# A gated long-convolution and spectral-filter kernel: a written-out order replaced, an output chunk kept in SBUF, zero matmuls ahead of the first data

## The chip, the cores and the metric

One core of a Trainium2 chip runs the whole program. TensorE (PE in the profile) does the matmuls, with its weight loads shown apart as PEld; VectorE (DVE), ScalarE (ACT) and GpSimd (POOL) work on tiles; SyncE (SP) issues most of the transfers, and GpSimd issues those that add to what DRAM already holds. The metric is the device time of one execution in microseconds; lower is better. The profile's times are counted from the start of the profiled span.

## The reference

Inputs are `q`, `k`, `v` and `x = q` of 2048 tokens by 640 channels (float32), and two branches are mixed by a gate of one number per token:

```python
def _A_ref(q, k, v, shift_k, ssm_k, ssm_D):
    k_shift = sum over t of k_pad[:, t:t + S, :] * shift_k[:, ks - 1 - t]   # 4 taps
    kv = k_shift * v
    y = irfft(rfft(kv, 2 * S) * rfft(ssm_k, 2 * S))[:S]     # long causal convolution, per channel
    return q * (y + kv * ssm_D)
def _B_ref(x, w_r, w_i):
    return irfft2(rfft2(x) * (w_r + 1j * w_i))               # over tokens and channels
g = _sigmoid((x * gate_w).sum(-1, keepdims=True))
return g * a + (1 - g) * b
```

## The kernel before

All transforms are matmuls with constant matrices. The 640 channels, in an order `PERM`, make five chunks of 128. The 2048 tokens are written as 64 x 2 x 16; a block `n` of 0 to 15 holds the 128 tokens with one last index, and blocks 0 to 7 and 8 to 15 are the two halves.

Branch B, in order: `dfwd(n)` loads a block of `xT`, folds it by symmetric channels (`fold`: sums and differences on DVE and POOL, one scaled copy on ACT) and multiplies by the channel matrix `dfc`, result in `XX`. Two unused columns of `dfc` are filled at run time by `gate_cols` with the gate's weights, so the same matmuls give the gate's sums; `gate` turns these into `g` and into `om`, which holds 1-g and g-1. `b1` and `bs2` are the two token steps forward with the product by `w`; `i1` the first step back; `bfin(n)` the last: matmuls `u` (L479, L485), a copy on ACT, matmuls `dic` (L497, L501). `bout(n)` scales by `om`, makes a sum (322 columns) and a difference (318) and sends the 128 x 640 block out.

Branch A, per chunk `c`: `kv` (four taps, transposes on PE, product with `v`), `s1` ("H" for the filter, "Y" for the data), `amid` (second step, product with the filter), `is1a` (first step back) and `afin(c, n0)` (last step back for one half of the blocks, product with `q*g`). The complex product of `amid` leaves four real products. `is1a` either takes all four as separate matmuls, or, for chunks in `SUMP`, `asum` first adds them in pairs on DVE or POOL and `is1a` has half the matmuls (`inv1`, L297).

The output of both branches is summed in DRAM. `FIRST` says, per half, from which chunk on branch B is the one that is written first. Before, `FIRST = (4, 5)`: chunks 0 to 3 of blocks 0 to 7, and all five chunks of blocks 8 to 15, are stored by `afin` and then added to by `bout` with GpSimd's accumulating transfer (L524); chunk 4 of blocks 0 to 7 is stored by `bout` (L522) and added to by `afin` (L681). An accumulating transfer waits until the store under it has landed.

Nothing is scheduled by the compiler. [...] There are 11 buffers `a`, 5 `s`, one `k`, one `kvt`, one `c1`, three `z` and the 8 PSUM banks.

Of the kernel before, what the change touches and what calls it, by code (L numbers as in the profile page):

```python
# [5 lines left out]
F32 = mybir.dt.float32  # L6
# [20 lines left out]
10/4/0 14/4 11 12 13 15 16 17 73+1/2/1 77/6 74+1 76+1 109+1/4/3 113/0 75+1 110+1 112<110 179/10 143 78 64+1/0/2 65+1 66+1 67<66 79 312/0 18/1 318/2  # L27
309/3 305/4 27/4 114 68/2 69 70 145+1/1/0 146+1 148<146 147 306 80 149/6 150 151 71 111 115 307 308/5 296/0 55/2/1 59/2 60 56 57+1 58+1 61 100+1/4/0
313 314/4/0 81/7 152 316/6 301/6 19/2/3 20 21 22+1<21 126/1 116 23/0 24 25 62 104/2 315 45/0 101 102 105 28/1/2 32/4 103+1 106 33 29+1<103 31+1 30+1
34 90/8 317 319+1 322/6 82/4/3 83 85 26 297/0 298 299 300/4 378/0 84 185/7 127/0/1 128 36/1 107 320/2 321 192/2 302/0/0 310/2 224/4 35 86/4 87 88 89  # L30
303 46/2/4 50/0 47 130 311 324/2/1 328/4 323 330/6 379/5 380/6 129 49 51 325 131/2 48 52 331 91/3/2 2 132 133 92+1 93+1 94+1 384/3 95/6 96 97 6 382/0
37/0/4 38 40 39 134 41/2 42 43 381<39 98 383 385 326/6 53 329 44 163/4 164 167/0 168 157/2 165/4 161/0 153 327 159/6 389/0 390/8 395/1 391/6 393/0 392
394 396 8/0 231/3 166 352/4 353/6 355+1 354+1 158 162 160 180/2 181/3/1 182 183 184 348/0 360/6 349/0 351 350 193/2 194/2/4 195 186/4 188/0/1 361/0
363+1 362 196+1 197<196 173/0 174 386/1 387/2/0 388 187/10 189 190+1 356/4 357/3 397/6 336/6 337/2 338 339+1<338 175/0 176 171/2 172 359 358 477/0
478/5 479/0 480 257/1 191 177/0 178 481/7 482 211/10 219/6 220/2/4 221 223 222 244/2 169/2 170 406/0 225/4 227/3/0 226/9 228 229 230 398/0 399 7 154/6
155 400/7 250/8 258/2 259/1/2 260 261 262 344/4 345/6 346+1 347+1 340/6 341/4 343 342 332/0 333/0 334 335 212/2 213/4 214/3/4 215 217 216 276/9 277/6
279/1/2 412/0/2 413 418/2 419 416/4 417 198/1 488/6 278/4 280+1 281<280 282 483/10 466/0 232/0 233/0/3 234 236+1 401+1<236 489+1 407+1 199/2 201/4/1
200/4 202+1 203<202 204 235 468/9 366/4 367 368/3 467/1 469 156 369 484 364/0 365 414/4 415 373/4 251/6 252/9 253/2/1 254 255 256 263/10 470/8 471 374
# [12 lines left out]
681+1 649 831 682/4/0 647 644/0 810 811 746/6/0/1 654 683 645 676 812/4 813 814 678/4 679 832+1/3 833<832 650/0 651 652 684/2 685 687+1 688/4 689
690/0 691 747 692/6/2 696/2 698/4 693 694/0 695 697 748/6 749 750 816/9 736/0/4/3 877/0 878 737 786/2/2/0 699 708/0 720/4 787 712/2 805 751 716/6
752+1/7 753+1 754 709/1 711 710 788/0 755 721/6 723+1<753 722 724/4 717/1 718 719 728/6 765 713/1 714+1<722 715 738/2 725/2 727 726 700/4 789 790 791
704/0 729/6 730 731 862/6/1/2 815 792/7<731 793 794 701/4 702 703 766/4/0/4 739 705/1 707 706 863 864/6 865 740 741 732/0 742/2<706 743 745 866 867
868+1/6 869+1 767 734/4 795 733 768/0 769 655/2 735 823/4 776/6/1/3 770 771 772+1/4 773<772 774 835/0/2/0 656 657 824 825 744 775 817 818/2 819 834
870 836 879 777 778/4 779 780 781 782+1/1 783<782 784 785 837/0 838 839 840 841/7 844/6/4/1 889/2/2/3 861 845 846/4 847 820 842+1 880/0/0/4 843 848
849 850/5<842 851 852 890 891/6 881 882/2 892 893 894 895+1/8 896<895 897 883 884 885 886+1/2 887<886 888
# [154 lines left out]
def _body(ctx, tc, I, out):  # L212
# [21 lines left out]
    def ps(b):  # L234
        return banks[:, b.slot:b.slot + b.banks]
# [38 lines left out]
    gs = cst.tile([128, 12], F32, name="gs")  # L274
# [30 lines left out]
    def gate_cols():  # L305
        unit("gcol")

        def calc():
            xv = gw.rearrange("p (u k) -> p u k", u=2)
            a, b = gs[:, 0:6], gs[:, 6:11]  # L310
# [500 lines left out]
```

## Time and profile before

| | |
|---|---|
| time, median of 3 runs | 312.15 us (310.73 to 313.74) |
| profiled execution: its time, its span | 312.69 us, 310.9 us |
| PE busy | 271.1 us, 87% of the span |
| DVE, POOL, ACT busy | 233.6, 186.8, 135.7 us |
| mean granted TensorE clock | 0.974 |
| DRAM read, written | 43.47 MB, 10.49 MB |
| of it by GpSimd's accumulating transfers | 5.24 MB |

Busy time is a share of the whole span and hides that stages differ; the view by windows gives it for one stretch. The chain of waits is followed back from the last instruction. In a timeline row stand start, length, engine, line, operation, output and inputs, the number of merged instructions, and in brackets how long the engine had been idle before it and who released it. A block's channel-transform matmul shows as x16 because each float32 matmul is two passes.

### The profile page before, as it was taken

What the parts mean: (1) busy time and instruction counts of PE and PEld (TensorE: products, weight loads), DVE (VectorE), ACT (ScalarE), POOL (GpSimd) and SP (SyncE); (2) the same over time, 40 slices, a digit from 0 to 9 for tenths busy, and PEclk for the clock granted to TensorE, in tenths of its full rate; (3) what the DMA queues carried; (4) which work ended last, traced back from release to release, by engine and by line L of the source; (5) the groups of instructions that cost most, each with busy time, mean ns of one, the idle gap of its engine ahead of it and who ended that gap; (6) DMA issues with size and microseconds to landing.
All of it is one profiled execution on the core that took longest, in us unless ns stands there. A gap on an engine that the chain in (4) does not pass through costs nothing. (4 is left out here: it accounts for less than half of the span.)

```text
span 310.9 us, 9643 instructions
## 1 busy us (share of the span) xinstructions
PE 271.1 (87%) x4196; PEld 167.7 (54%) x4196; DVE 233.6 (75%) x293; ACT 135.7 (44%) x229; POOL 186.8 (60%) x171
## 2 busy tenths in 40 slices
PE   0779999999989979979899899899999999999900
PEld 0556657455454345624337576476755767488700
DVE  2578898489979899965899888987789777665230
ACT  2154537614462652466652465766270354033300
POOL 3326794978898798949869615525943154123491
PEclk9999999999999999989999999999999999999965
DMA  7998769525684437959322950004553370436996
GB/s 235 409 409 330 288 214 404 214 69 165 186 278 147 159 103 242 265 205 383 121 95 80 317 186 0 11 2 136 175 189 108 73 99 17 70 89 130 181 130 108
DMA packets 25418, 54.58 MB, mean 176 GB/s; under 512 B 1824, under 2 KB 13344, under 8 KB 24864
## 3 DMA queue, kind: packets, MB, share of 16 engines
q1 hardware_dynamic: 22032, 48.72, 46.0%
q0 software_dynamic: 3344, 5.24, 11.4%
q8 instruction: 33, 0.54, 0.7%
q14 instruction: 9, 0.07, 0.1%
HBM read 43.47 MB, written 10.49 MB: 174 GB/s over the span
## 5 line engine op out<-in xcount | busy, mean ns | idle before, releaser
L559 POOL TENSOR_TENSOR a<-a,a 128x1024 f32<-128x1024 f32 x24 | 57.1, 2380 | 10.1 <-ACT XX L378 4.7
L593 DVE STREAM_TRANSPOSE ZZ<-banks 128x1024 f32<-128x1024 f32 x40 | 47.8, 1228 | 3.4 <-PE banks L590 3.3
L616 PE MATMUL banks<-ZZ,s2a 64*32 64x256 f32 x1280 | 41.4, 389 | 3.8 <-issue 1.7
L553 ACT ACTIVATE a<-k,one 128x1024 f32<-128x1024 f32 x32 | 34.9, 1141 | 13.5 <-DMA k<-k 10.1
L633 POOL TENSOR_TENSOR ZZ<-a 128x512 f32<-128x512 f32 x19 | 24.3, 1290 | 16.9 <-ACT a L625 11.2
L363 PE MATMUL banks<-dfc,s 128*64 128x162 f32 x256 | 22.8, 324 | 12.0 <-DVE dfc L321 9.8
L616 PEld LDWEIGHTS banks<-ZZ,s2a 64*32 64x32 f32 x1280 | 24.2, 105 | 16.8 <-issue 2.9
L297 PE MATMUL banks<-ZZ,one 32*64 32x512 f32 x512 | 30.9, 605 | 0.7 <-DVE ZZ L593 0.4
L631 DVE TENSOR_TENSOR ZZ<-banks,s 128x512 f32<-128x512 f32 x40 | 25.4, 685 | 7.9 <-ACT s L627 7.7
L302 DVE STREAM_TRANSPOSE ZZ<-banks 128x2048 f32<-128x2048 f32 x10 | 23.0, 2312 | 7.4 <-PE banks L297 7.4
L363 PEld LDWEIGHTS banks<-dfc,s 128*64 128x64 f32 x256 | 17.7, 145 | 17.0 <-POOL s L338 9.8
L458 POOL TENSOR_TENSOR XX<-s,s 128x320 f32<-128x320 f32 (+1 forms) x29 | 24.2, 856 | 4.5 <-DVE s L452 2.8
L625 ACT ACTIVATE a<-banks 128x1024 f32<-128x1024 f32 x20 | 20.3, 1024 | 14.9 <-DVE XX L422 7.1
L524 POOL DMA_DIRECT2D out_dram<-a x16 | 15.1, 1022 | 18.5 <-DMA out_dram<-a 10.4
L513 ACT ACTIVATE s<-banks,om 128x322 f32<-128x322 f32 x16 | 8.5, 530 | 39.6 <-PE banks L501 27.5
L518 POOL TENSOR_TENSOR a<-s 128x318 f32<-128x318 f32 x13 | 12.8, 987 | 20.1 <-issue 9.4
L515 DVE SCALAR_TENSOR_TENSOR s<-banks,om,s 128x322 f32<-128x322 f32 x32 | 17.3, 544 | 9.2 <-ACT s L513 8.6
L664 ACT ACTIVATE a<-a,g 128x128 f32<-128x128 f32 x80 | 24.2, 392 | 0.0
L627 ACT ACTIVATE s<-banks 128x512 f32<-128x512 f32 x20 | 12.0, 598 | 23.5 <-PE banks L616 21.2
L501 PE MATMUL banks<-dic,s 128*128 128x161 f32 x128 | 21.9, 313 | 0.0
L501 PEld LDWEIGHTS banks<-dic,s 128*128 128x128 f32 x128 | 18.0, 189 | 7.1 <-issue 7.1
L297 PEld LDWEIGHTS banks<-ZZ,one 32*64 32x64 f32 x512 | 12.9, 129 | 15.6 <-issue 12.9
(73 smaller groups left out, 491.6 us busy)
## 6 DMA issues: line engine op xcount, KB each, us to landing
a<-xT SPq DMA_DIRECT2D x16, 512.0 KB, 7.4
k<-k SPq DMA_DIRECT2D x10, 704.0 KB, 5.9
a<-h SPq DMA_DIRECT2D x10, 544.0 KB, 3.7
a<-w SPq DMA_DIRECT2D x16, 322.0 KB, 3.9
a<-v SPq DMA_DIRECT2D x10, 512.0 KB, 4.8
a<-q SPq DMA_DIRECT2D x10, 512.0 KB, 4.8
out_dram<-a SPq DMA_DIRECT2D x9, 512.0 KB, 3.7
out_dram<-a POOLq DMA_DIRECT2D x8, 320.0 KB, 6.2
```

The source lines that it names most:

```text
L297: mm(p[h * 64:h * 64 + 64, j, :nd * 8], is1[r, c, :], v[r, h * 2 + ri, :, d0:d0 + nd, :].rearrange("p m d e -> p d m e"), start=(i == 0), ...
L302: nc.vector.transpose(by_col(x, d0, nd), p[:, :, :nd * 8].rearrange("p j (d i) -> p d j i", i=8))
L363: mm(v[ri * 64:ri * 64 + 64, z, o], fv[:, i, t], dfc[:, i, :], start=(b == 0), stop=True, tile_position=(0, ri * 64), skip_group_check=True)
L458: either(2 * nc_, lambda q, ri=ri, o=o, dst=dst: q(dst(), T(t1)[:, :, ri], T(t2)[:, :, 1 - ri], op=o), r=[t1, t2], w=[("XXp", z, i, ri)])
L501: mm(ps(p)[:, k, r * 161:r * 161 + 161], sb(u, 5, 128)[:, k * 2 + r], dic[:, (k * 2 + r) * 161:(k * 2 + r) * 161 + 161], start=False, stop ...
L553: tap = lambda t, j: op([("ACT", act_us(1024), lambda: act(sb(t, 8, 128), K(j), AF.Copy, scale=sh[:, c, j:j + 1]))], r=[k, "one"], w=[t], ...
L559: either(1024, lambda o, t=t: o(sb(acc, 1024), sb(acc, 1024), sb(t, 1024), op=OP.add), r=[t], w=[acc])
L593: op([("DVE", dve(1024), lambda: nc.vector.transpose(by_col(Z(z), u * 32, 32), ps(p).rearrange("p b (d n) -> p d b n", n=16)))], r=[p], w= ...
L616: mm(ps(p)[j * 32:j * 32 + 32, h].rearrange("p (y r d) -> p y r d", y=2, r=2)[:, :, ri], s2a[r, k, ri * 32:ri * 32 + 32], ZZ[r, a:b + 1:b ...
L631: alts = [("DVE", dve(512), lambda x=x, dst=dst, hv=hv: tt(dst(), V(part(ps(p), zy)), hv(), op=OP.mult))]
L633: alts.append(("POOL", pool_us(512), lambda x=x, dst=dst, hv=hv: ptt(dst(), V(part(sb(hs, 2, 512), zy)), hv(), op=OP.mult)))
L664: act(sb(qt, 8, 128)[:, j], sb(qt, 8, 128)[:, j], AF.Copy, scale=g[:, n0 + j:n0 + j + 1])
```

## The change

- `FIRST` becomes (4, 4), with `KEEP = (1,)`: branch B no longer adds to chunk 4 of blocks 8 to 15 in DRAM. `bout` leaves these 128 columns of each of the eight blocks in one SBUF tile (`keep`), and the last `afin` takes the product with `q*g` in two halves of 512 columns, adds the kept columns, and stores. To make the kept columns one operation, `PERM` is rearranged and the difference is split into 190 and 128 columns.
- `SUMP` becomes (2, 3, 4): the products of chunk 4 are summed too.
- `warm`: 14 matmuls of a zeroed 128x128 tile stand first on PE; nothing uses their result.
- `gate_cols` writes into `dfc` directly; the factor 0.25 moves into the sigmoid's scale. `gate` makes 1-g as a second sigmoid and g-1 as a scaled copy, all on ACT.
[...]

```diff
-PERM = np.array(list(range(161)) + list(range(320, 481)) + [640 - d for d in range(1, 160)] + [320 - d for d in range(1, 160)])
-FIRST = (4, 5)
-FWD, INV, SUMP = 1, 1, (2, 3)
+PERM = np.array(list(range(161)) + list(range(320, 481)) + [b - d for lo, hi in ((1, 96), (96, 160)) for b in (640, 320) for d in range(lo, hi)])
+FIRST = (4, 4)
+FWD, INV, SUMP = 1, 1, (2, 3, 4)
+WARM = 14
+KEEP = (1,)
 TABLE = """
-117/0 1 0 118+1/0/1 119<118 4 122/0 123 120 121 135/1 136/2/3 140/2 137 139 3 5 124 125 141 9/2 72/3 108/4 63/5 138+1 142 304/0 54/6 144/7 99/8 218/9
+10/0 3 0 2 1/0 5 64/1 118/2 55/3 28/4 312/5 109/6 91/7 304/0 11/0/1 127/8 12 100/9 15/2 46/10 14 136/0 13+1<14 16 6 17 65+1/2/3 66+1 69/4 309/1 67+1
...
-            tt(b[:, 0:2], a[:, 0:6:4], a[:, 1:6:4], op=OP.add)
-            tt(b[:, 2:4], a[:, 0:6:4], a[:, 1:6:4], op=OP.subtract)
-            stt(b[:, 4:5], a[:, 3:4], sg, a[:, 2:3], op0=OP.mult, op1=OP.add)
-        op([("DVE", 0.7, calc)], r=["one", "two"], w=["gs"])
-        def put():
...
+            tt(w[:, 0:323:322], a[:, 0:6:4], a[:, 1:6:4], op=OP.add)
+            tt(w[:, 484:487:2], a[:, 0:6:4], a[:, 1:6:4], op=OP.subtract)
+            for r, j in ((slice(0, 64), 0), (slice(64, 128), 160)):
+                stt(dfc[r, 4, j:j + 1], a[r, 3:4], sg[r], a[r, 2:3], op0=OP.mult, op1=OP.add)
+        op([("DVE", 1.5, calc)], r=["one", "two"], w=["dfc"])
...
-        op([("ACT", 1.5, lambda: act(g, ps(p)[:, 0, :16], AF.Sigmoid))], r=[p], w=["g"])
         def f():
-            nc.vector.tensor_scalar(om[:, 0], g, -1.0, 1.0, op0=OP.mult, op1=OP.add)
-            nc.vector.tensor_scalar(om[:, 1], g, 1.0, None, op0=OP.subtract)
-        op([("DVE", 0.25, f)], r=["g"], w=["om"])
+            act(g, ps(p)[:, 0, :16], AF.Sigmoid, scale=0.25)
+            act(om[:, 0], ps(p)[:, 0, :16], AF.Sigmoid, scale=-0.25)
+            act(om[:, 1], om[:, 0], AF.Copy, scale=-1.0)
+        op([("ACT", 1.9, f)], r=[p], w=["g", "om"])
...
+        either(190, lambda q: dif(q, yn()[:, 322:512], 1, 96), r=rr, use=[ab, y], w=[(y, 1)])
+        if keep:
+            either(128, lambda q: dif(q, sb(keep, 8, 128)[:, n % 8], 96, 160), r=rr, use=[ab, keep], w=[(keep, n)], new=[] if keep in made else [keep])
...
+        fin = c == NCH - 1 and n0 // 8 in kept
+        for i in range(2 if fin else 1):
+            m = 512 if fin else 1024
...
+        if c == NCH - 1 and keep:
+            for i in range(2):
+                r = slice(i * 4, i * 4 + 4)
+                either(512, lambda o, r=r: o(sb(qt, 8, 128)[:, r], sb(qt, 8, 128)[:, r], sb(keep, 8, 128)[:, r], op=OP.add), "DVE", ...)
+                load(lambda r=r: dma(out[:, n0 + r.start:n0 + r.stop, c, :], sb(qt, 8, 128)[:, r]), 262, r=[(qt, "y", i)], use=[qt])
...
+    unit("warm")
+    op([("DVE", 0.2, lambda: nc.vector.memset(wrm, 0.0))], w=["wrm"])
+    pw = new("ps")
+    def warm():
+        for _ in range(WARM):
+            mm(ps(pw)[:, 0, :128], wrm, wrm, start=True, stop=True)
+    pe(6.0, warm, "F", r=["wrm"], w=[pw], new=[pw])
```

Since the table tells nothing by itself, three places in the order follow. In the changed kernel's rows the lines have moved by a few numbers: L596 is the old L590, L571 the old L565, L302 the old L297 on PE, L681 the old L675, L476/L482 the old `u`, L494/L498 the old `dic`, L530 the old L524, L699 the old L681.

The first loads on SP, before:

```order
L332 DMA a_63<-xT 128x1024
L282 DMA two<-two 128x129
L282 DMA one<-one 128x476
L332 DMA a_64<-xT 128x1024
L282 DMA dfc<-dfc 128x972
L332 DMA a_65<-xT 128x1024
```

and in the changed kernel:

```order
L328 DMA a_63<-xT 128x1024
L287 DMA two<-two 128x129
L287 DMA one<-one 128x476
L287 DMA dfc<-dfc 128x972
L328 DMA a_64<-xT 128x1024
L328 DMA a_65<-xT 128x1024
```

The channel matrix `dfc`, which the first matmul needs, has changed places with the second block of `xT`.

The end of PE's list, before: `u` of block 15, `dic` of 10, `u` of 14, `dic` of 15 and 14, all of the second half.

```order
L479 MATMUL banks<-c_79,XX 128x2x64 x4
L485 MATMUL banks<-c_79,XX 32x64 x8
L497 MATMUL banks<-dic,s_78 128x322 x2
L501 MATMUL banks<-dic,s_78 128x161 x4
L479 MATMUL banks<-c_79,XX 128x2x64 x4
L485 MATMUL banks<-c_79,XX 32x64 x8
L497 MATMUL banks<-dic,s_76 128x322 x2
L501 MATMUL banks<-dic,s_76 128x161 x4
L497 MATMUL banks<-dic,s_74 128x322 x2
L501 MATMUL banks<-dic,s_74 128x161 x4
```

In the changed kernel, after the last half of chunk 4's `is1a`: `dic` of block 12, `u` of 14 and 13, `afin(4, 0)` (L681), `dic` of 13 and 14, `afin(4, 8)`:

```order
L494 MATMUL banks<-dic,s_74 128x322 x2
L498 MATMUL banks<-dic,s_74 128x161 x4
L476 MATMUL banks<-c_79,XX 128x2x64 x4
L482 MATMUL banks<-c_79,XX 32x64 x8
L476 MATMUL banks<-c_79,XX 128x2x64 x4
L482 MATMUL banks<-c_79,XX 32x64 x8
L681 MATMUL banks<-ZZ,is2a 64x128 x16
L494 MATMUL banks<-dic,s_74 128x322 x2
L498 MATMUL banks<-dic,s_74 128x161 x4
L494 MATMUL banks<-dic,s_78 128x322 x2
L498 MATMUL banks<-dic,s_78 128x161 x4
L681 MATMUL banks<-ZZ,is2a 64x128 x16
```

Chunk 4's `afin` of blocks 8 to 15 has moved from the middle of the blocks to the very end.

The end of POOL's list, before: adds of the last blocks alternate with the accumulating transfers.

```order
L524 DMA out_dram<-a_73 128x640
L681 DMA out_dram<-a_72 128x8x128
L524 DMA out_dram<-a_70 128x640
L517 TENSOR_TENSOR a_68<-s_75 128x322
L518 TENSOR_TENSOR a_68<-s_75 128x318
L524 DMA out_dram<-a_68 128x640
L518 TENSOR_TENSOR a_71<-s_77 128x318
L524 DMA out_dram<-a_71 128x640
L518 TENSOR_TENSOR a_65<-s_78 128x318
L524 DMA out_dram<-a_65 128x640
```

and in the changed kernel:

```order
L530 DMA out_dram<-a_71 128x512
L530 DMA out_dram<-a_64 128x512
L699 DMA out_dram<-a_67 128x8x128
L516 TENSOR_TENSOR a_65<-s_77 128x128
L516 TENSOR_TENSOR a_73<-s_75 128x190
L530 DMA out_dram<-a_73 128x512
L530 DMA out_dram<-a_63 128x512
L516 TENSOR_TENSOR a_65<-s_76 128x128
```

Each accumulating transfer has 512 columns instead of 640, two stand behind the last `afin` add (L699) instead of four, and the last POOL row fills the kept tile (`a_65` here).

More of the change, by code (lines that the diff above doesn't have):

```diff
@@ L273, in _body @@
     g = cst.tile([128, 16], F32, name="g")
[L274 removed]
+    gs = cst.tile([128, 8], F32, name="gs")
+    wrm = cst.tile([128, 128], F32, name="wrm")
     om = cst.tile([128, 2, 16], F32, name="om")
@@ L466, in i1 @@
         op([("DVE", dve(nd * 32), lambda: back4(XX, ps(p), d0, nd))], r=[p], w=[("XXi", u)])
+    kept, made = {h: new("a") for h in KEEP}, set()
     def bfin(ns, is2b_buf):
@@ L510, in bout @@
         c1 = FIRST[n // 8]
+        keep = kept.get(n // 8)
         av = lambda: sb(ab, 2, 2, 161)
@@ L517, in bout @@
         either(322, lambda q: q(sb(y, 2, 161), av()[:, :, 0], av()[:, :, 1], op=OP.add), r=[(ab, 0), (ab, 1)], use=[ab], w=[(y, 0)], new=[y])
-        either(318, lambda q: q(sb(y, 640)[:, 322:].rearrange("p (a c) -> p a c", a=2), av()[:, :, 0, 1:160], av()[:, :, 1, 1:160], op=OP.subtract),
-               r=[(ab, 0), (ab, 1)], use=[ab, y], w=[(y, 1)])
-        yv = lambda lo, hi: sb(y, NCH, 128)[:, lo:hi]
-        if c1 < NCH:
-            load(lambda: dma(out[:, n, c1:, :], yv(c1, NCH)), 65 * (NCH - c1), r=[(y, 0), (y, 1)], use=[y], w=[("o", c, n // 8, n) for c in range(c1, NCH)])
+        dif = lambda q, o, lo, hi: q(o.rearrange("p (a c) -> p a c", a=2), av()[:, :, 0, lo:hi], av()[:, :, 1, lo:hi], op=OP.subtract)
+        yn = lambda: sb(y, 640)
+        rr = [(ab, 0), (ab, 1)]
+        either(190, lambda q: dif(q, yn()[:, 322:512], 1, 96), r=rr, use=[ab, y], w=[(y, 1)])
+        if keep:
+            either(128, lambda q: dif(q, sb(keep, 8, 128)[:, n % 8], 96, 160), r=rr, use=[ab, keep], w=[(keep, n)], new=[] if keep in made else [keep])
+            made.add(keep)
+        else:
+            either(128, lambda q: dif(q, yn()[:, 512:640], 96, 160), r=rr, use=[ab, y], w=[(y, 2)])
+        yv = lambda lo, hi: sb(y, 640).rearrange("p (c d) -> p c d", d=128)[:, lo:hi]
+        ys = [(y, i) for i in range(2 if keep else 3)]
+        if c1 < NCH and not keep:
+            load(lambda: dma(out[:, n, c1:, :], yv(c1, NCH)), 65 * (NCH - c1), r=ys, use=[y], w=[("o", c, n // 8, n) for c in range(c1, NCH)])
         if c1:
             op([("POOL", 1.0, lambda: nc.gpsimd.dma_start(out[:, n, :c1, :], yv(0, c1), accum_op=OP.add))],
-               r=[(y, 0), (y, 1)] + [("o", c, n // 8, n) for c in range(c1)], use=[y], kb=130 * c1)
+               r=ys + [("o", c, n // 8, n) for c in range(c1)], use=[y], kb=130 * c1)
     def kv(c, h, kvt):
```

82 lines of the change are left out of this document (41 added, 41 removed).

## The prediction

> **What bounds the kernel now.** I read the page's shares first, then the chain that ended last, then windows cut where PE's work changes, then the timeline at both ends.
>
> ```profile
> span 310.9 us, 9643 instructions
> PE 271.1 (87%) x4196; PEld 167.7 (54%) x4196; DVE 233.6 (75%) x293; ACT 135.7 (44%) x229; POOL 186.8 (60%) x171
> PE 27%; POOL 5%; DMA 3%; issue 2%; DVE 2%; POOLq 0%; ACT 0%; ACTq 0%; DVEq 0%
> ```
>
> PE is busy for 87% of the span, and PE has the largest share of the chain, which reaches back only to 176.96 us. Where the other 13% lie shows by stages (columns: window, its length, busy time of PE, PEld, DVE, ACT, POOL, granted clock, DMA share, GB/s):
>
> ```profile
> 9.79:56.24 46.45, 43.93 (x560) 30.07 (x560) 35.63 (x64) 22.94 (x36) 25.87 (x30) 1.00 0.89 344
> 56.24:130.00 73.76, 67.91 (x1186) 36.79 (x1192) 66.09 (x73) 33.52 (x49) 63.04 (x52) 1.00 0.56 175
> 130.00:176.00 46.00, 42.00 (x737) 21.89 (x724) 37.38 (x34) 25.13 (x38) 35.21 (x25) 0.96 0.56 191
> 176.00:240.00 64.00, 61.26 (x900) 39.13 (x901) 53.85 (x63) 32.43 (x68) 31.53 (x28) 1.00 0.34 110
> 240.00:296.05 56.05, 56.04 (x826) 39.74 (x822) 35.41 (x50) 19.63 (x35) 19.63 (x23) 1.00 0.53 96
> 4.36:298.53 294.17, 271.14 (x4196) 167.66 (x4196) 233.58 (x293) 135.73 (x229) 181.88 (x162) 0.99 0.57 177
> ```
>
> The first matmul starts at 9.79, the last ends at 296.05. In between PE lacks 2.5 + 5.9 + 4.0 + 2.7 + 0.0 = 15.1 us; it is 95% busy, and the granted clock stays at 1.00 but for 0.96 in one window. So the span is 9.8 of lead-in + 271.1 of matmuls + 15.1 of PE waits + 14.9 after the last matmul. This sum is the profiled execution's: 310.9 of span in a time of 312.69, 1.8 around it; the median of the runs is 0.5 lower than that execution.
>
> The lead-in and the end:
>
> ```profile
> 2.59 0.43 SPq L282 DMA_DIRECT2D dfc<-dfc  x1
> 7.72 1.26 POOL L337 TENSOR_TENSOR s<-a 128x512 f32<-128x512 f32 x1 [0.38 <-DMA a<-xT]
> 8.95 1.03 DVE L321 TENSOR_SCALAR dfc<-gs 128x2 f32<-128x2 f32 x4 [1.20 <-DMA dfc<-dfc]
> 9.79 2.43 PE L363 MATMUL banks<-dfc,s 128*64 128x162 f32 x16 [9.79 <-DVE dfc L321]
> 12.14 1.36 PE L372 MATMUL banks<-dfc,s 64*64 64x162 f32 x16
> 13.43 1.90 PE L363 MATMUL banks<-dfc,s 128*64 128x162 f32 x16
> 15.26 0.78 PE L372 MATMUL banks<-dfc,s 64*64 64x162 f32 x16
> 15.97 1.32 PE L363 MATMUL banks<-dfc,s 128*64 128x162 f32 x16
> ...
> 276.78 1.23 DVE L678 TENSOR_TENSOR a<-banks,a 128x1024 f32<-128x1024 f32 x1 [0.62 <-PE banks L675]
> ...
> 284.53 2.64 POOL L524 DMA_DIRECT2D out_dram<-a  x3 [7.59 <-DMA out_dram<-a]
> ...
> 290.50 1.10 PE L479 MATMUL banks<-c,XX 128*128 128x128 f32 x8
> 291.89 0.81 PE L497 MATMUL banks<-dic,s 64*128 64x322 f32 x4
> 293.93 0.81 PE L497 MATMUL banks<-dic,s 64*128 64x322 f32 x4
> 294.68 1.37 PE L501 MATMUL banks<-dic,s 128*128 128x161 f32 x8
> 303.28 0.86 POOL L524 DMA_DIRECT2D out_dram<-a  x1 [0.30 <-POOL a L518]
> ```
>
> At the start DVE waits for `dfc` (1.20 us, ended 8.95), then PE for DVE. The first matmul groups run slow: 2.43 and 1.36, then 1.90, where the same groups later take 1.32 and 0.78. At the end POOL stood still for 7.59 us, until 284.5, for a store to land. The chain of waits names it:
>
> ```profile
> 276.78 1.24 DVE a L678
> 278.03 5.95 DMA out_dram<-a
> ```
>
> It is chunk 4's `afin` of blocks 8 to 15, whose product (L678) ends at 278.0. The eight blocks of that half may be added only on top of it, since all five of their chunks are added in DRAM. So eight accumulating transfers, one of the first half and the last `afin`'s (3.4 MB) are left for the time after 284.5, and the last of them is issued at 303.28, 7 us after PE has ended. PE's end alone does not set the end: PE could stop earlier and this queue would still have to drain.
>
> **The change part by part.** *Start of PE.* Ahead of `dfc` and with it stand 512 + 64 + 238 + 512 + 486 = 1,812 KB on SP; without the second `xT` 1,300 KB. That much (1,326 KB, the second `xT` as fourth transfer) had landed at 7.72, when POOL began on it. Then four small instructions on `dfc`, as now: 8.95 to 9.79, 0.84 us. First matmul at 8.6: **-1.2**; bounds 0 (the landing is set by latency) and -1.5.
>
> *Zero matmuls.* They stand ahead of everything on PE and wait only for a memset on DVE.
>
> ```profile
> L479 PE MATMUL banks<-c,XX 128*128 128x128 f32 x128 | 18.8, 290 | 0.0
> ```
>
> In this group a 128x128 matmul is two passes, x128 for 64 matmuls in 18.8 us, 0.29 each; at the slow rate 2.43/1.32 times as much, 0.53. PE was slow for 5.5 us (9.79 to 15.26), so ten slow ones and four of 0.29, 6.5 us from about 1.1 on: done at 7.6, before the data. Slow groups saved: 1.11 + 0.58 + 0.58 = **-2.3**; bounds 0 (slow again by 8.6, or it is not activity that ends the slowness) and -2.3. All slow they would end at 8.6, so they cost nothing.
>
> *Third chunk summed.*
>
> ```profile
> 191.53 3.94 PE L297 MATMUL banks<-ZZ,one 32*64 32x512 f32 x64
> 263.50 7.35 PE L297 MATMUL banks<-ZZ,one 32*64 32x512 f32 x128
> L640 DVE TENSOR_TENSOR ZZ<-ZZ 128x512 f32<-128x512 f32 x5 | 3.3, 689 | 0.3
> L631 DVE TENSOR_TENSOR ZZ<-banks,s 128x512 f32<-128x512 f32 x40 | 25.4, 685 | 7.9 <-ACT s L627 7.7
> L627 ACT ACTIVATE s<-banks 128x512 f32<-128x512 f32 x20 | 12.0, 598 | 23.5 <-PE banks L616 21.2
> ```
>
> `is1a` of chunk 3, summed, takes 3.94; of chunk 4, not summed, 7.35: **-3.4**; bounds 0 (below) and -3.7 (half of it). Eight adds come in, five on DVE (0.69) and three on POOL, all beside PE. What has to come in time is the chain behind the last `amid`: ACT's copy 0.60, two products of 0.69, two adds of 0.69, 3.4 us on two engines that also serve the blocks. Between that `amid` and `is1a` PE's list has three `u` (290.50 to 291.89, 1.4 each) and three `dic` (291.89 to 293.93, 2.0 each): 10 us of cover. With the cover gone the chain would cost its 3.4 and the gain would be nil.
>
> *Early order.* Four `amid` and one `kv` of PE's work (5.2 us) now stand ahead of the first `b1`, and with them about 9 us of DVE work.
>
> ```profile
> L593 DVE STREAM_TRANSPOSE ZZ<-banks 128x1024 f32<-128x1024 f32 x40 | 47.8, 1228 | 3.4 <-PE banks L590 3.3
> ```
>
> By the order's rows it is five products like L631 (3.4), one more transpose (1.2) and a `kv` product and the gate's sum, taken as long as it (2.4), and two adds of 1,024 columns, for which the trace has no row on DVE; I take twice L640's 0.69 each (2.8); less the gate's instructions. DVE was free for 46.45 - 35.63 = 10.8 us in that window, so it fits, narrowly. Walking the order with the rows' durations, PE waits for DVE at the second, the seventh and the eighth block of `dfwd`, 1.2 + 0.5 + 1.6 = 3.3 us where all waits of the window are 2.5 now, and I add as little again before the `amid` products, which need ACT and DVE in turn. **+1.0**; bounds 0 (it fits) and +9 (none of it does).
>
> *The end.* Now 14.9 us from PE's end, T. In the changed order the second half's accumulating transfers wait only for chunk 3's `afin`; behind that stand nine `u` and ten `dic` on PE, 33 us by the rows above, besides chunk 4's last steps. What is left for the end is `afin(4, 8)` with its kept columns and two plain stores, and the transfers of the last two blocks.
>
> ```profile
> L513 ACT ACTIVATE s<-banks,om 128x322 f32<-128x322 f32 x16 | 8.5, 530 | 39.6 <-PE banks L501 27.5
> L515 DVE SCALAR_TENSOR_TENSOR s<-banks,om,s 128x322 f32<-128x322 f32 x32 | 17.3, 544 | 9.2 <-ACT s L513 8.6
> out_dram<-a SPq DMA_DIRECT2D x9, 512.0 KB, 3.7
> out_dram<-a POOLq DMA_DIRECT2D x8, 256.0 KB, 4.9
> ```
>
> The last `dic` ends about 2.0 before T (one `afin`, 16 matmuls of 128 columns, behind it); ACT 0.5, two L515 1.1, two adds 0.9: T + 0.5. Product, add, product, add of 512 columns at 0.69: T + 3.3. Issue 0.4, landing 3.7: T + 7.4, and 0.4 from there to the span's end. Beside it the last accumulate is issued by T + 1.4 and takes 4.9 to land. End at T + 7.8, **-7.1**. One bound is -9 (the store of half the size lands in 2, the adds overlap PE); the other 0: 3.4 MB of accumulates take the 26 us after 284.5 now, 130 GB/s, and the last four transfers of the new list, 1.3 MB, would take 10 us if they all came late, which with a landing of 4.9 is as long as now.
>
> *Small edits.* 1-g on ACT (0.6 us of ACT, 44% busy) takes two instructions from DVE; the gate columns lose three. Nothing, hidden by PE's work between `gate` and the first use of `om`. If ACT were late, 0.6.
>
> *The middle.* Another order between 56 and 240 us, where PE now lacks 12.6. By the order's counts DVE's work grows from 233.6 to about 241: five adds of L640's kind (+3.4), four adds of 1,024 columns that POOL had (+5.5), the cut differences and sums (+4.9), the last `afin`'s adds (+1.4); six L631 go to POOL (-4.1), the gate's instructions go (-3.6). POOL's falls by 4, ACT's stays. Six `i1` now stand in a row, where `is1a` broke them up, with a DVE transpose behind each. I see no place where the waits must grow or shrink and take **0**; bounds -6 (half the waits) and +9 (DVE's 7 us at its share of 79%).
>
> Sum: 310.9 - 1.2 - 2.3 + 1.0 - 3.4 - 7.1 = 297.9; + 1.8 - 0.5 gives **299 us**. Its own range, by the bounds of the start and the end, is 294 to 306.
>
> **The rivals.** *DVE sets the pace, and it is not faster.* DVE works 233.6 of the 294.2 us between its first and last instruction, 79.4%. My forecast has it work 241 of 289, 83%; it reaches 90% in 56:130 and 84% in 176:240, but never over the whole. At 79.4% it needs 303.5, and with 4.4 ahead, 4.8 behind and 1.3 around the time is 314; past 315.3, over 1% slower, once its share is below 79.0%. What could hold it there is POOL:
>
> ```profile
> L517 DVE TENSOR_TENSOR a<-s x9: 486/496/1198, 204.1 to 297.3; 128x322 f32<-128x322 f32 x9
> 297.33 1.20 DVE L517 TENSOR_TENSOR a<-s 128x322 f32<-128x322 f32 x1
> 297.09 2.03 POOL L518 TENSOR_TENSOR a<-s 128x318 f32<-128x318 f32 x1
> ```
>
> An add with two SBUF inputs took 1.20 instead of 0.50 where POOL was adding, and POOL's beside it 2.03. Of such DVE adds in the output part and the sums there are 38 instead of 17; if all 21 meet POOL, 14.7 us more, and 317 even at 83%. Against: the median of nine stayed at 0.50. [...] *The end stays.* The accumulates end the run as now: 299 + 7 = 306. For: they land in order behind one another and POOL issues them all. Against: they may start more than 33 us before T. *The new order closes waits too.* Half of the 12.6 gone, and the end at its best: 291. For: nothing but that the waits are many and small. *The change does not do what it says*: the zeros are done early and PE is slow again: 301, inside the forecast's range.
>
> **How the numbers follow.** Forecast 0.62 (with the cold zeros), the end stays 0.13, closed waits 0.12, DVE's pace 0.13. About 1%, 3.1 us, can be told from no change: faster is below 309.0, slower above 315.3. Forecast, closed waits and the end stays are faster (0.87, of which 0.01 spills over); DVE's pace splits evenly around 315: same 0.07, slower 0.07. The range 290 to 309 leaves out DVE's pace and the outermost of the closed waits, under 2 in 10.
>
> **What would show it.** First dfc matmul at 8.6 and its first two groups at 1.3 and 0.8; first `b1` at 58 to 60; the ZZ group of `is1a` at x448 instead of x512; PE's end near 290; span end 8 us after it, with a plain store last. PE waits above 20 us in sum, or DVE above 85% with PE waiting for it, would say that the middle was wrong; a last row on POOL more than 10 us after PE's end that the end was.

## The result and the profile after

| | before | after |
|---|---|---|
| time, median (runs) | 312.11 us (4: 310.73 to 313.74) | 303.96 us (4: 303.71 to 304.87) |
| ratio, 95% interval | | 0.9742 (0.9691 to 0.9794) |
| profiled span | 310.9 | 301.8 |
| first matmul on data | 9.79 | 8.38 (predicted 8.6) |
| PE's matmuls from there on | 271.1 | 268.3 (265.4) |
| PE's waits from there to its end | 15.1 | 16.9 (16.1) |
| after PE's last matmul | 14.9 | 8.2 (7.8) |

A later measurement of the changed kernel, beside other variants, gave 301.53 us (six runs, 300.08 to 303.87), ratio 0.9702 (0.9655 to 0.9749). The change makes the kernel faster; 299 was 5 us too low against the first measurement and 2.5 against the second, inside the range of 290 to 309 both times.

The page of the changed kernel, busy times:

```profile
span 301.8 us, 9609 instructions
PE 273.1 (90%) x4160; PEld 169.9 (56%) x4160; DVE 242.1 (80%) x310; ACT 136.1 (45%) x231; POOL 184.3 (61%) x177
```

PE's 273.1 hold 4.7 of zero matmuls. DVE has 242.1 where 241 were forecast. By windows (columns as before: busy time of PE, PEld, DVE, ACT, POOL, granted clock, DMA share, GB/s):

```profile
8.38:58.80 50.42, 46.96 (x696) 32.01 (x697) 43.24 (x71) 26.17 (x42) 27.44 (x32) 1.00 0.91 351
58.80:130.00 71.20, 66.14 (x1083) 35.84 (x1081) 60.80 (x64) 36.66 (x54) 55.40 (x46) 0.98 0.53 168
130.00:166.46 36.46, 34.16 (x636) 18.17 (x629) 33.10 (x37) 18.67 (x32) 30.35 (x23) 1.00 0.73 223
166.46:188.00 21.54, 18.31 (x277) 6.90 (x272) 19.25 (x13) 13.04 (x30) 21.18 (x16) 1.00 0.36 136
188.00:216.00 28.00, 25.31 (x440) 19.12 (x437) 21.31 (x28) 10.54 (x15) 13.87 (x11) 0.94 0.46 154
216.00:293.61 77.61, 77.43 (x1022) 53.29 (x1020) 59.39 (x88) 29.33 (x59) 33.83 (x45) 1.00 0.47 74
```

From 216 on PE has almost no waits (0.2 us). The window 188 to 216 is the odd one by its clock: 0.94, with 2.7 us of waits. Start and end in the timeline:

```profile
1.06 4.74 PE L710 MATMUL banks<-wrm 128*128 128x128 f32 x28 [1.06 <-DVE wrm L705]
8.38 1.34 PE L359 MATMUL banks<-dfc,s 128*64 128x162 f32 x16 [2.58 <-DVE dfc L319]
9.65 0.78 PE L368 MATMUL banks<-dfc,s 64*64 64x162 f32 x16
11.94 1.93 PE L359 MATMUL banks<-dfc,s 128*64 128x162 f32 x16 [1.51 <-DVE s L341]
14.51 1.32 PE L359 MATMUL banks<-dfc,s 128*64 128x162 f32 x16
58.80 13.71 PE L414 MATMUL banks<-XX,two 128*128 128x512 f32 x32
...
291.57 2.04 PE L681 MATMUL banks<-ZZ,is2a 128*64 128x128 f32 x32
293.99 0.86 POOL L530 DMA_DIRECT2D out_dram<-a  x1 [0.47 <-DVE a L516]
295.07 1.78 SPq L697 DMA_DIRECT2D out_dram<-a  x2
```

The zeros were done at 5.8 (7.6 forecast), the first block's groups took 1.34 and 0.78 as forecast, and then PE waited 1.51 us for the second block's data. That block's first group took 1.93, no less than the 1.90 of before. The first `b1` starts at 58.80 (forecast 58 to 60). At the end the last accumulating transfer is issued at 293.99, where it was 303.28, and two plain stores come last.

### The profile page after: what moved, and what is told of

The parts are those of the page before. It is cut to its first block, busy times and chain, and to the rows that moved or that the text cites. A ratio compares the mean times of both kernels' runs of the same rounds, so it can differ in the third digit from the quotient of the medians.

```text
span 301.8 us, 9609 instructions
## 1 busy us (share of the span) xinstructions
PE 273.1 (90%) x4160; PEld 169.9 (56%) x4160; DVE 242.1 (80%) x310; ACT 136.1 (45%) x231; POOL 184.3 (61%) x177
## 4 chain that ended last, share of the span: by engine, by line
PE 42%; DVE 9%; DMA 2%; POOL 2%; issue 2%; ACT 1%; POOLq 0%; ACTq 0%; DVEq 0%
PE banks L302 7%; PE banks L622 7%; PE banks L498 6%; PE banks L476 5%; PE banks L681 5%; PE banks L596 4%; PE banks L494 3%; DVE ZZ L307 2%; DVE XX L307 2%; DMA a<-w 2%; PE banks L482 2%; DVE ZZ L599 1%; PE banks L571 1%; PE banks L433 1%; DVE ZZ L637 1%
## 5 line engine op out<-in xcount | busy, mean ns | idle before, releaser
L565 POOL TENSOR_TENSOR a<-a,a 128x1024 f32<-128x1024 f32 x20 | 47.6, 2386 | 12.6 <-DVE ZZ L646 5.8
L639 POOL TENSOR_TENSOR ZZ<-a 128x512 f32<-128x512 f32 x25 | 31.9, 1295 | 30.0 <-ACT a L631 17.8
L559 ACT ACTIVATE a<-k,one 128x1024 f32<-128x1024 f32 x32 | 36.0, 1146 | 21.9 <-DMA k<-k 8.3
L302 PE MATMUL banks<-ZZ,one 32*64 32x512 f32 x448 | 27.4, 608 | 1.6 <-ACT a L442 1.1
L453 POOL TENSOR_TENSOR XX<-s,s 128x322 f32<-128x322 f32 (+1 forms) x28 | 23.3, 851 | 4.4 <-DVE s L447 2.1
L487 ACT ACTIVATE s<-banks 128x640 f32<-128x640 f32 x16 | 11.3, 705 | 32.0 <-PE banks L482 30.4
L445 DVE TENSOR_TENSOR s<-banks,a 128x640 f32<-128x640 f32 (+1 forms) x24 | 18.9, 814 | 6.0 <-ACT a L442 2.9
L498 PEld LDWEIGHTS banks<-dic,s 128*128 128x128 f32 x128 | 18.6, 195 | 7.5 <-issue 7.5
L498 PE MATMUL banks<-dic,s 128*128 128x161 f32 x128 | 22.5, 319 | 0.0
L646 POOL TENSOR_TENSOR ZZ<-ZZ 128x512 f32<-128x512 f32 x14 | 17.8, 1290 | 5.8 <-DVE ZZ L646 3.2
L596 PE MATMUL banks<-kvt,one 64*128 64x512 f32 x80 | 20.1, 617 | 0.5 <-DVE ZZ L307 0.5
L596 PE MATMUL banks<-a,one 64*128 64x512 f32 x80 | 19.6, 609 | 0.9 <-POOL a L565 0.8
```

The costliest lines, as they stand in the source:

```text
L302: mm(p[h * 64:h * 64 + 64, j, :nd * 8], is1[r, c, :], v[r, h * 2 + ri, :, d0:d0 + nd, :].rearrange("p m d e -> p d m e"), start=(i == 0), ...
L498: mm(ps(p)[:, k, r * 161:r * 161 + 161], sb(u, 5, 128)[:, k * 2 + r], dic[:, (k * 2 + r) * 161:(k * 2 + r) * 161 + 161], start=False, stop ...
L559: tap = lambda t, j: op([("ACT", act_us(1024), lambda: act(sb(t, 8, 128), K(j), AF.Copy, scale=sh[:, c, j:j + 1]))], r=[k, "one"], w=[t], ...
L565: either(1024, lambda o, t=t: o(sb(acc, 1024), sb(acc, 1024), sb(t, 1024), op=OP.add), r=[t], w=[acc])
L596: mm(ps(p)[:, b], m1[r], v[r], start=True, stop=True)
L639: alts.append(("POOL", pool_us(512), lambda x=x, dst=dst, hv=hv: ptt(dst(), V(part(sb(hs, 2, 512), zy)), hv(), op=OP.mult)))
```

## The experiments

Times stand beside the kernel before on the same chip, six runs of each variant. Unless said otherwise an edit is made to the changed kernel alone. In `TABLE` an operation is a number; the list is the order in which operations are put out, and each engine takes its own in that order. `+1` takes the second of the allowed engines, `/` gives the buffers, and `n<m` makes operation `n`, on DVE or POOL, wait for `m` on the other of the two: 40 hand-set waits in the changed kernel, 32 before.

**Without the zeros.**

```diff
-WARM = 14
+WARM = 1
```

Expected: 

> The changed kernel with 1 zero matmul instead of 14. Theory: the zeros save almost nothing, because the second block's data set the pace: its last fold product ends at 11.9 whatever PE did before. Without zeros the first block's groups take 2.4 and 1.4 again and end at 12.1, the wait of 1.51 before the second block is gone, the second block runs slow (1.9, as it does now), and the third block starts at 14.7 instead of 14.51: time 304.2, between +0 and +0.6. Rival, the prediction's term: the slow groups come back in full, +2.3, 306.3.

Measured: 301.31 us (297.92 to 302.62), ratio 0.9655 (0.9598 to 0.9711). PE's timeline:

```profile
8.68 2.44 PE L359 MATMUL banks<-dfc,s 128*64 128x162 f32 x16 [6.83 <-DVE dfc L319]
11.05 1.36 PE L368 MATMUL banks<-dfc,s 64*64 64x162 f32 x16
12.34 1.84 PE L359 MATMUL banks<-dfc,s 128*64 128x162 f32 x16
14.82 1.32 PE L359 MATMUL banks<-dfc,s 128*64 128x162 f32 x16
```

The first block is slow again, the wait before the second is gone, and the third block starts 6.14 us after the first matmul (14.82 - 8.68); with the zeros it was 6.13 (14.51 - 8.38). The zeros moved nothing past the second block. The time is 2.9 below the 304.2 expected, which was reckoned from the first measurement of the changed kernel; against the later one it is 0.2 lower.

**The sums of chunk 4 without their use on PE.**

```diff
-([] if c in SUMP else [(2, h, 1), (1, h, 0)])
+([] if c in SUMP and c < NCH - 1 else [(2, h, 1), (1, h, 0)])
```

Expected: 

> The changed kernel, but is1a of chunk 4 takes four products again as separate matmuls, while the sums are still made (so that chunk of the output is not the reference's). Theory, the prediction's term: PE has no wait there, so the two halves take 3.4 to 4.1 us more in sum (four groups of 2.05 instead of two) and the end moves by as much: 307.4 to 308. Rival: the end is set by DVE or by the transfers, and the time stays within 1 us of 304.

Measured: 305.84 us (302.57 to 308.63), ratio 0.9800 (0.9740 to 0.9861), 4.3 above the later measurement of the changed kernel and 1.9 above the first, and below the 307.4 to 308 expected. The six runs lie up to 6 us apart, and the profiled one is the slowest of them; without it the median is 304.82. The trace is narrower. PE from the first `is1a` half of chunk 3 to its last group, in this kernel:

```profile
219.28 2.04 PE L302 MATMUL banks<-ZZ,one 32*64 32x512 f32 x32
296.83 2.04 PE L681 MATMUL banks<-ZZ,is2a 128*64 128x128 f32 x32
```

and in the changed kernel, from the same half to the 291.57 shown above:

```profile
217.47 2.04 PE L302 MATMUL banks<-ZZ,one 32*64 32x512 f32 x32
```

77.55 against 74.10 us: 3.45 for the four-product form, with nothing around it that hides it; the granted clock is 1.00 over this stretch in both traces.

**The end alone, in the kernel before.**

```diff
-out[:, n, :c1, :], yv(0, c1)     r=... for c in range(c1)
+out[:, n, :m, :], yv(0, m)       r=... for c in range(m)      # m = min(c1, 4)
```

Expected: 

> The kernel before, but the accumulating transfers of blocks 8 to 15 carry chunks 0 to 3 only (branch B is missing from chunk 4 of these blocks), so they no longer wait for the store of chunk 4's afin. Everything else stays. Theory, the prediction's: POOL's wait of 7.59 us until 284.5 goes, PE's end stays at 296, the end comes 8 to 11 us after it: time 304.5 to 307. Rival: POOL's second wait, 3.95 us until 294.9 for a plain store of chunk 4, swallows the gain, and the list behind it is worked off one by one: 310 to 311.

Measured: 305.70 us (304.04 to 307.78), ratio 0.9821 (0.9764 to 0.9877). POOL and PE at its end (L525 is L524 of before, L682 its L681):

```profile
278.73 2.64 POOL L525 DMA_DIRECT2D out_dram<-a  x3 [3.26 <-DMA out_dram<-a]
287.48 1.87 POOL L682 DMA_DIRECT2D out_dram<-a  x1
297.55 0.86 POOL L525 DMA_DIRECT2D out_dram<-a  x1 [0.30 <-POOL a L518]
...
293.21 1.37 PE L501 MATMUL banks<-dic,s 128*128 128x161 f32 x8
```

The three transfers that stood until 284.5 go at 278.7, what remains of the wait is 3.3 us for another store, the second wait (3.95 until 294.9) is gone with the first, and the last transfer is issued at 297.55 instead of 303.28. PE ends at 294.6, the span at 303.1: 8.5 behind it. The theory of the store under the accumulates holds, the rival falls. That these transfers are also a fifth shorter is in the 6.4 us by which the time falls, and was not tried apart.

**Without one hand-set wait.** `665` is POOL's add of the last tap in chunk 4's first `kv`, `637` a sum of chunk 3 on DVE.

```diff
-665<637
+665
```

Expected: 

> The changed kernel without one of the 40 hand-set waits between DVE and POOL: the last tap's add of chunk 4's first kv on POOL no longer waits for a sum of chunk 3 on DVE. Theory: the add runs at 204.8 to 207.2 instead of 209.1 to 211.5, PE's wait of 1.85 us before the transposes at 211.53 goes, and the slow groups behind it (1.43, 1.45, 1.98 instead of 1.03, 0.81, 1.37) run at the full rate: 300.5, 3.4 less. Rival: the next product is late instead (DVE's transposes and products of that stage), and the time stays at 303 to 304.

Measured: 300.06 us (298.91 to 300.42), ratio 0.9630 (0.9591 to 0.9670). The changed kernel at that place, POOL and PE (idle time and releaser in brackets):

```profile
206.99 1.18 PE L622 MATMUL banks<-ZZ,s2a 64*32 64x256 f32 x32
209.10 2.37 POOL L565 TENSOR_TENSOR a<-a,a 128x1024 f32<-128x1024 f32 x1 [5.83 <-DVE ZZ L646]
211.53 1.43 PE L571 MATMUL banks<-one,a 128*128 128x128 f32 x8 [1.85 <-POOL a L565]
212.88 1.45 PE L494 MATMUL banks<-dic,s 64*128 64x322 f32 x4
```

and without the wait:

```profile
204.06 2.35 POOL L565 TENSOR_TENSOR a<-a,a 128x1024 f32<-128x1024 f32 x1 [1.74 <-ACT a L559]
209.69 0.66 PE L571 MATMUL banks<-one,a 128*128 128x128 f32 x4 [0.28 <-DVE s L513]
210.28 0.81 PE L494 MATMUL banks<-dic,s 64*128 64x322 f32 x4
```

The wait closed a ring. DVE's sum needs the products of the `amid` that PE runs at 206.99; POOL's add, whose data were there at 204.8 (ACT's copy, 203.64 to 204.78), started behind that sum at 209.10; and PE's transposes stood behind the add. PE waited for what followed from its own matmul, and was slow afterwards. The windows over these groups (the clock is the third column from the right), with the wait:

```profile
211.53:216.08 4.55, 4.55 (x21) 3.35 (x22) 3.81 (x5) 0.35 (x1) 3.32 (x4) 0.62 0.02 5
```

and without it:

```profile
209.69:213.96 4.27, 4.00 (x40) 3.13 (x41) 4.17 (x7) 0.68 (x2) 1.66 (x2) 1.00 0.02 4
```

The clock is 0.62 with the wait and 1.00 without it in these two traces. The same kernel once more, beside the last two variants below:

> The changed kernel without the one hand-set wait, once more, as the measure for the two runs beside it: 299 to 300.5.

Measured: 300.37 us (299.43 to 303.01), ratio 0.9656 (0.9601 to 0.9712). By the medians the wait costs 1.2 to 3.9 us against the two measurements of the changed kernel, and the interval of the later one overlaps with both of this kernel. The traces are narrower. From the `amid` at that place to PE's end it is 86.6 us in the first profile of the changed kernel (206.99 to 293.61) and 86.5 in the later one, and 83.8 in both profiles of the kernel without the wait, so the wait costs 2.7 to 2.8. The rest of PE's stretch differs between executions by other things. The profile of the kernel with `dfc` put back (below) divides the cost. It still has the hand-set wait, and PE waits the same 1.85 us, but the groups behind it run fast:

```profile
206.68 1.13 PE L622 MATMUL banks<-ZZ,s2a 64*32 64x256 f32 x32
211.17 1.09 PE L571 MATMUL banks<-one,a 128*128 128x128 f32 x8 [1.85 <-POOL a L565]
212.20 0.81 PE L494 MATMUL banks<-dic,s 64*128 64x322 f32 x4
```

There it is 84.9 from the `amid` to PE's end. So about 1.1 of the 2.8 us are the wait itself, and some 1.7 the slow groups that follow it in the other four profiles that have it.

**The changed kernel again**, with three others.

> The changed kernel itself, as it is, timed beside the next three and the kernel before on one chip. If the kernels' own spread from execution to execution is what let the one without zeros come out at 301.3 (297.9 to 302.6), this one gives 301 to 305 with a median near 304, and no run under 300; if that was a difference of the two chips, it gives 301 to 302.

Measured: 301.53 us, the later measurement told above. So the distance between the kernel without zeros (301.31) and the first measurement (303.96) need not be an effect of the zeros. By the expectation's own rule this is a difference of the chips; but the kernel before stood at 312.11 and 311.31 us in the two measurements, so what made the first one 2.4 higher stays open.

**Without the zeros and without that wait** (`WARM = 1`, `665`).

> The changed kernel with 1 zero matmul instead of 14, and without the hand-set wait that held the last tap's add of chunk 4's first kv on POOL. If the zeros are worth their predicted 2.3, 302.4. If they are worth nothing, because what PE gains before the second block is lost at the next data and in later waits, 299.5 to 300.5, as with zeros. If they cost something, because later waits fall into place by the shift as in the trace of the kernel without zeros alone (73.4 instead of 75.8 between two same points of the middle), 297 to 298.

Measured: 298.29 us (296.20 to 300.04), ratio 0.9583 (0.9539 to 0.9626). By the median that is the fastest of all kernels here, ahead of both the kernel before and the changed one. Its interval and that of the kernel with zeros and without the wait overlap, so it is not shown that the zeros cost something; a gain of 2.3 by them does not fit any of the four measurements.

**`dfc` behind the second block again** (`5 64/1` in the table becomes `64/1 5`).

> The changed kernel with the order of the loads as before: the second block of xT ahead of dfc. The prediction's term: the first matmul 1.2 later, at 9.6, and the time 1.2 longer, 305.2. Theory: the second block's folds come 1 us earlier in exchange, so that its matmuls start right behind the first block's, at 11.7 to 12.0, the third block starts as now at 14.5, and the time stays at 303.5 to 304.5.

Measured: 303.02 us (301.61 to 305.41), ratio 0.9750 (0.9702 to 0.9799), 1.5 above the changed kernel beside it, with overlapping intervals. My theory that it costs nothing fell in the trace:

```profile
9.57 2.44 PE L359 MATMUL banks<-dfc,s 128*64 128x162 f32 x16 [2.75 <-DVE dfc L319]
15.18 1.32 PE L359 MATMUL banks<-dfc,s 128*64 128x162 f32 x16
```

The first matmul is 1.2 us later than in the changed kernel's first profile, as predicted, its group is slow in spite of the zeros, and the third block starts at 15.18 where the changed kernel had 14.51 and, in its later profile, 14.01. One pair of traces would not carry this, since the first matmul moves from execution to execution: in the ten profiles with `dfc` early it lies between 7.42 and 8.68, in the three with `dfc` late (this one and the two of the order before) between 9.30 and 9.79. The two groups do not meet, and their means are 1.5 us apart.

**Without any hand-set wait** (all 40 `<n` struck out of the table).

> The changed kernel without any of its 40 hand-set waits between DVE and POOL (the data waits stay). If meetings of DVE and POOL cost as in single rows (a DVE add of 0.50 took 1.20), 40 more meetings at 0.7 lengthen DVE's work by up to 28 us, and the time goes to 306 or more. If the median row holds and such meetings mostly cost nothing, DVE's and POOL's work stays within 3 us of what it is, the wait before 211.53 goes as in the kernel without that one wait, and the time is 299 to 301.

Measured: 303.56 us (301.39 to 304.65), ratio 0.9744 (0.9703 to 0.9785): 3.2 and 3.5 us above the two measurements of the kernel that lacks one wait only (the interval is clear of the first and just touches the second), and 2.0 above the changed kernel beside it, with overlapping intervals. DVE's busy time rose from 242.1 to 251.5, POOL's from 184.3 to 191.1. DVE's adds of two taps (min/median/max in ns) in the changed kernel:

```profile
L565 DVE TENSOR_TENSOR a<-a,a x4: 1186/1212/1226, 49.7 to 95.6; 128x1024 f32<-128x1024 f32 x4
```

and here:

```profile
L565 DVE TENSOR_TENSOR a<-a,a x4: 1180/1488/2140, 50.4 to 96.3; 128x1024 f32<-128x1024 f32 x4
```

The sign of the rival is right, its size is not: 9.4 us more on DVE, not 28. The other 39 waits as a whole earn their place; with the one that costs 2.8 among them, it is not shown that the 40 do.

**Zeros in the waits** (22 zeros ahead, and 7 behind the first and the seventh block, without the wait of `665`).

```diff
+            if ns[0] in (0, 9):
+                for _ in range(7):
+                    mm(ps(pz[0])[:, 0, 324:384], wrm, wrm[:, :60], start=True, stop=True, skip_group_check=True)
```

Expected: 

> The changed kernel without the one hand-set wait before chunk 4's transposes, with 22 zero matmuls ahead of the first data instead of 14, and 7 short zero matmuls (60 columns) right behind the first and the seventh block, in the waits of 1.5 and 1.7 us there. If it is idle time that makes PE slow, the first, second and eighth block's first groups all take 1.32 to 1.34 (second block 1.93 and eighth 1.71 to 2.4 so far), and from the first matmul to the first b1 it takes 49.4 instead of 50.4 to 52.2; the time 299.0. Rival: the slow stretches come at these places all the same, or the gain before b1 is lost in later waits: 300.

Measured: 300.51 us (299.57 to 301.62), ratio 0.9665 (0.9612 to 0.9717), the same as without them; from the first matmul to the first `b1` it takes 51.7 us, not 49.4. The rival came.

```profile
10.43 1.77 PE L372 MATMUL banks<-wrm 128*128 128x60 f32 x14
12.13 1.84 PE L359 MATMUL banks<-dfc,s 128*64 128x162 f32 x16
26.60 1.77 PE L372 MATMUL banks<-wrm 128*128 128x60 f32 x14
30.06 1.32 PE L359 MATMUL banks<-dfc,s 128*64 128x162 f32 x16 [1.69 <-DVE s L341]
```

The second block's group takes 1.84 right behind running matmuls, so idle time is not what stretches it. And the wait before the eighth block did not shrink, it moved back by the 1.77 of the zeros. ACT in the changed kernel shows why:

```profile
26.62 0.75 ACT L374 ACTIVATE XX<-banks 128x648 f32<-128x648 f32 x1
27.26 0.37 ACT L340 ACTIVATE banks<-s,two 128x128 f32<-128x128 f32 x1
```

It copies the seventh block out of PSUM as soon as PE is done with it (26.56), and only then scales a piece of the ninth's folds (L340), behind which DVE's last step for the eighth stands. That wait starts from PE's own end. The zeros stand in the same operation as the block, ahead of what lets ACT go (with them PE ends it at 28.37, which is 26.60 + 1.77), so they push the wait back instead of filling it.

**The eighth block's folds first.**

```diff
-132/2 102+1 99 129+1 130+1 318/4 301/5 37/6 103+1 145/7 73/9 105/4 131<103 106 133 134
+132/2 129+1 99 130+1 133 318/4 301/5 37/6 131<130 134 102+1 103+1 145/7 73/9 105/4 106
```

Expected: 

> The changed kernel without the one hand-set wait before chunk 4's transposes; besides, DVE finishes the folds of the eighth block in PE's order before those of the ninth (three rows moved), and POOL's fold of that block waits for one DVE row less. The wait of 1.73 us ahead of the eighth block becomes 0.5 to 0.7. Theory: what comes earlier before b1 arrives at the end: 298.5 to 299. Rival: the middle takes it back, 300.

Measured: 299.41 us (298.03 to 299.79), ratio 0.9610 (0.9562 to 0.9658), 1.0 below the kernel it starts from, with overlapping intervals: neither theory is settled. The wait became 0.75 + 0.43, not 0.5 to 0.7:

```profile
27.22 0.49 PE L359 MATMUL banks<-dfc,s 128*64 128x162 f32 x2 [0.75 <-DVE s L341]
28.14 1.31 PE L359 MATMUL banks<-dfc,s 128*64 128x162 f32 x14 [0.43 <-POOL s L337]
```

Here the trace parts the group: one matmul in its two passes, a wait for POOL's fold, then the rest at full speed. In the changed kernel the same wait lies inside the group (28.29, 1.71 long, POOL's fold from 27.90 to 28.62) and looks like slow matmuls.

## Why the prediction was right or wrong

**Start of PE, -1.2: right.** Measured -1.4 in the first matmul, 1.5 by the means of all profiles and, by the kernel with `dfc` put back, 0.7 to 1.2 at the third block.

**Zero matmuls, -2.3: wrong, 0.** The step that failed is "Slow groups saved: 1.11 + 0.58 + 0.58". The first two groups were saved, the time was not: the second block's data set the next start, and a faster first block only waits longer. The third group was not even saved: it took 1.93 where 1.32 was forecast, because POOL's fold for it ended inside. My walk of the order had this wait in it (1.2 at the second block), and I booked it to the order instead of to the zeros.

**Early order, +1.0: wrong by -2.1, and right with the zeros by luck.** From the first matmul to the first `b1` there were 46.45 us before and 5.2 of work came in; forecast 46.45 + 5.2 - 2.3 + 1.0 = 50.35, measured 50.42. Waits were forecast at 3.5 and are 50.42 - 46.96 = 3.46. But the kernel without zeros and without the wait takes 50.53 for the same stretch, 1.1 less than 46.45 + 5.2: the order alone shortened it by about 1.1 us and the zeros by nothing. Two errors of about 2 us cancelled. (That +1.0 does not follow from its rows either: 3.3 - 2.5 is 0.8, and "as little again" would make 1.6.) The close match is of one profile, too: the later one of the same kernel takes 52.2, with slow groups at the eighth block. Two terms that share a wait cannot be priced one by one.

**Third chunk summed, -3.4: right.** 3.45 by the trace.

**The end, -7.1: right.** 14.9 became 8.2, -6.7, and the kernel before with only that dependency cut falls by 6.4 in time. That the accumulating transfers land in order, the ground for the rival, is so in the trace of before (the ten issued from 284.53 to 303.28 landed one after another, from 288.8 to 309.4); but waiting for chunk 4's store was the cause, with the shorter transfers' share not parted from it; the wait of 3.95 us that stood behind it in the queue was its consequence.

**Small edits, 0:** not tried alone; ACT's work is 136.1 against 135.7.

**The middle, 0: wrong by +3.6, inside its bounds of -6 and +9.** From the first `b1` to PE's end it took 239.8 us (56.24 to 296.05), less 5.2 and 3.4 makes 231.2; measured 234.8 (58.80 to 293.61). The step that failed is "I see no place where the waits must grow or shrink". One place could have been seen in the order's rows: a POOL add on the way to PE that is tied to a DVE sum that comes from PE. By the stretch from the `amid` on, that wait and the slow groups behind it are 2.8 of the 3.6; what the other 0.8 are stays open. Without that one wait PE ends at 290.0 (forecast "near 290") and the profiled span is 297.9, which is the forecast's sum. That it meets the sum so closely is partly luck: 0.7 of the 3.5 us by which PE's stretch is shorter there lie ahead of the wait's place, and the errors of the zeros and the order cancel in it too.

**DVE's pace, the rival at 314: did not come, and the reason given was half right.** DVE was at 80%, and PE's waits grew by 1.8 in all. Yet the argument "the median of nine stayed at 0.50" leaned on rows of a kernel whose order keeps such meetings apart; with the waits struck out DVE works 9.4 us longer. One place in the traces: in the changed kernel POOL stands still beside DVE's add of two taps at 95.58 (1.21 us) and goes on behind it, at 97.02; of the same four DVE adds without the waits the longest took 2.14.

**What would show it.** First matmul, first two groups, `b1` and the 8 us of the end came as written, and the ZZ group fell to x448; PE's end came 3.6 late, most of it by the one wait, and the sum of waits (16.9) stayed under the mark of 20. PE's matmuls came out 2.9 above the forecast (268.3 against 265.4): 0.6 and 0.4 of it are the waits for POOL inside the second and the eighth block's groups, and some 1.7 the slow groups behind the hand-set wait.

## What to carry to other kernels

Ask of each saved stretch what is late next: a faster first block gains nothing when the second block's data are on their own clock. Look through hand-set waits for rings, where an engine waits for something that starts from its own last result; one in 40 cost 2.8 us here, most of what PE's stretch missed. And where an accumulating transfer has to follow a store, count the queue behind it: here a landing of 6 us and what queued behind it cost some 6.5 at the end.

## What the runs showed of the hardware

*A stretched matmul group is not always a slow clock.* The second and eighth block's groups (1.93, 1.71) hold a wait for a POOL fold inside. The two folds in the changed kernel:

```profile
11.77 0.73 POOL L337 TENSOR_TENSOR s<-s 128x256 f32<-128x256 f32 x1 [4.85 <-DVE s L334]
27.90 0.72 POOL L337 TENSOR_TENSOR s<-s 128x256 f32<-128x256 f32 x1 [1.65 <-DVE s L336]
```

The groups end 1.37 and 1.38 us behind them (at 13.87 and 30.00), and in both PE's weight loads stand still for POOL's fold after the first two, 0.42 us until 12.55 and 0.23 until 28.68. With the zeros in the waits, where PE comes straight from other matmuls, 14 of the second block's 16 rows run in 1.31 us, from 12.66 on, as those behind POOL's fold do in the variant with the eighth block's folds first. Over the eighth block the granted clock tells the two cases apart. The windows over it in the changed kernel:

```profile
28.29:30.63 2.34, 2.34 (x32) 1.65 (x32) 2.23 (x5) 1.09 (x2) 0.34 (x1) 1.00 0.99 404
```

and over the same place in its later profile:

```profile
27.79:33.00 5.21, 5.21 (x52) 3.65 (x52) 4.60 (x10) 2.57 (x4) 2.17 (x4) 0.67 1.01 379
```

At the start the clock's row cannot be read so. The kernel without zeros, from its first matmul on:

```profile
8.68:14.82 6.14, 6.12 (x64) 4.44 (x64) 5.41 (x15) 1.52 (x3) 0.73 (x1) 1.00 1.02 408
```

It shows 1.00 although the first group took 2.44 instead of 1.32. The prediction's first window, 9.79 to 56.24, shows 1.00 over such slow groups as well.

*The same wait is followed by slow matmuls in one execution and not in another.* Both stretches follow a wait of 1.73 us, in the same program. In the later profile the groups are slow:

```profile
27.79 2.36 PE L359 MATMUL banks<-dfc,s 128*64 128x162 f32 x16 [1.73 <-DVE s L341]
```

For this block and the next PE took 5.87 us there (27.79 to 33.66) and 4.31 in the first profile (28.29 to 32.60). Of the ten profiles with a wait of 1.69 to 1.73 at this place three have slow groups behind it; of the five with 1.85 or 1.86 ahead of chunk 4's transposes, four. So a wait of 1.73 us was followed by a clock of 0.67 here and of 1.00 in the first profile, and one of 1.85 us by 0.62 in the first profile and by groups at full speed (1.09, 0.81) with `dfc` put back. What decides it in a given execution stays open.
